# Loading half of the gate's rows early, and moving a quarter of the modal spectrum into the second convolution

## The chip, the cores and the metric

The kernel runs on one core of one Trainium2 chip. The metric is device time in microseconds (us), the median of several executions. The engines are named as the profile names them: PE is TensorE, DVE VectorE, ACT ScalarE, POOL GpSimd and SP SyncE, whose instruction queue issues most of the DMAs.

## The reference

Two layers alternate on x, a sequence of L = 2048 steps with D = 512 channels, twice: A (H3), B (S4D), A, B. Both end in a long causal convolution in each channel, done as a multiplication in the frequency domain with 4096 points.

```python
def _A_ref(q, k, v, shift_k, ssm_k, ssm_D):
    # k_shift: causal convolution of k with 4 taps
    kv = k_shift * v
    y = irfft(rfft(kv, 2*S) * rfft(ssm_k, 2*S))[:S] + kv * ssm_D
    return q * y

def _B_ref(u, log_A_real, A_imag, C_real, C_imag, log_dt, D_skip):
    dt = exp(log_dt); A = -exp(log_A_real) + 1j * A_imag; C = (C_real + 1j * C_imag) * dt
    K = 2.0 * einsum("dn,dnl->dl", C, exp((A * dt) * pos)).real      # the taps, from N = 128 modes
    return irfft(rfft(u, 2*L) * rfft(K, 2*L))[:L] + u * D_skip

x = A_q
x = x + _A_ref(layernorm(x), A_k, A_v, A_shift_k, A_ssm_k, A_ssm_D)
x = x + _B_ref(layernorm(x), B_log_A_real, ..., B_D_skip)
x = x + _A_ref(layernorm(x), A_k, ...)       # the same y as the first time
x = x + _B_ref(layernorm(x), B_log_A_real, ...)
```

Since k and v of layer A are given, its y is the same both times: it is computed once, kept in DRAM (`ya_d`), and each A layer is only an update x = x + layernorm(x) * y.

## The kernel before, in words

Work is cut into 4 quarters of 128 channels (`NQ`) and, in the frequency domain, 8 chunks (`NCH`) per quarter, so that a convolution has 32 steps. A convolution by matmuls goes through these tiles: a first stage of the transform (`fwd_group`: `pf` from `u` or `kk`, L174), a transpose in blocks of 32 on DVE into `zu` or `zk` (L192, L194), a second stage (`f2_chunk`: `pu`, L199), the product with the spectrum `kab` (ACT makes a swapped copy `sw`, L284 and L285; DVE multiplies into `vv`, L286; POOL multiplies `sw`, L288, and adds, L289; every third add is DVE's), a first inverse stage four steps later (`pi`, L298, copied to `ie` by ACT, L299), a transpose into `w` (L313), and a second inverse stage eight steps after that (`po`, L319).

The spectra that these products need are made by the same stages. `spectrum_quarter` makes one quarter of a spectrum: four loads `kk` with a forward group each, then eight chunks that ACT copies from `pu` into `pc` (L250) and SP stores to `spec` in DRAM (L251). It is a generator: each `next` runs one forward group or one chunk. Spectrum 0 belongs to layer A. Spectrum 1, the modal one, belongs to layer B; its taps come from the modes (`taps`: angles, sines `co` on ACT, products `xye`, a contraction on PE, `pk`), which go by way of `kdram` (L549) to `kk`.

The program has three parts that matter here. First, `diagonal()` (spectrum 0 and the convolution of layer A, which stores `ya_d`, L684) runs interleaved with `stream()` (the taps and spectrum 1). Where group 16, 32, 48 or 64 of the taps is contracted, the quarter of spectrum 1 that is then complete is put into the list `todo`, which `stream()` works off. Second, `gated_update` for the first A layer: it loads x (L729) and the rows `yaq` of `ya_d` (L732, in two pieces, groups 0 to 11 and 12 to 15, for the first three of four row blocks), makes `ut` = 1 + y * rs on ACT (L743), updates x on DVE (L754), and takes statistics of the new rows on DVE for the first eight row tiles and as squares on ACT (L760) for the last eight. `normalizer` turns them into `rs` and `nb` with a square root on ACT (L216, behind a load of an activation table) and a short chain on DVE (L217 to L222). Third, the convolution of layer B, `conv_b(0)`: `u` is the normalised x (L817 on ACT, others on DVE), and steps 0 to 31 follow.

Within one engine the instructions run in a fixed order, which the framework's scheduler sets when the program is built; a step of a generator that is written earlier tends to come earlier on every engine. DMAs stand in the queue of the engine that issues them (SP for most, POOL for `kk` of the last quarter and the first two `kab`).

Of the kernel before, what the change touches and what calls it, by code (L numbers as in the profile page):

```python
# [9 lines left out]
F32 = mybir.dt.float32  # L10
# [91 lines left out]
def kernel(ctx: ExitStack, tc: tile.TileContext, out, x_in, kv_in, ssmk_in, ssmd_in,  # L102
# [122 lines left out]

    def spectrum_quarter(which, q, src, pool, zlast, zb, tag):
        z = pool.tile([128, 64, 32, 2], F32, name="zk", tag="z", bufs=zb) if which else z_of_a()
        dr = pool.tile([1, 128], F32, name="dr", tag="dr", bufs=1)
        nc.sync.dma_start(dr, (ssmd_in, dsk_in)[which][:, 128 * q:128 * q + 128])
        for g in range(4):  # L230
            kk = pool.tile([128, 512], F32, name="kk", tag="kk", bufs=3 - which)
            (G if which and q == NQ - 1 else nc.sync).dma_start(kk, src[4 * q + g])
            d = dr[:, 32 * g:32 * g + 32]
            if which == 0:
                kv = kk.rearrange("p (t c) -> p t c", c=32)
                view = lambda ps_, j, n: kv[ps_, :, j:j + n]
            else:
                kv = kk.rearrange("p (i t c) -> p t i c", i=4, c=8)
                view = lambda ps_, j, n: kv[ps_, :, j // 8:(j + n) // 8, :]
                d = d.rearrange("p (i c) -> p i c", c=8)  # L240

            G.tensor_add(kv[0:1, 0], kv[0:1, 0], d)
            fwd_group(view, z, 32 * g, 32, 32 if "f1" in psum else 16, zlast[-zb] if len(zlast) >= zb else None, full="f1" not in psum)
            yield
        for c in range(NCH):
            pu, ins = f2_chunk(z, c, None, tag)
            if c == NCH - 1:
                zlast.append(ins)
            pc = pool.tile([128, CK * 128], F32, name="pc", tag="pc", bufs=2 + 2 * which)
            last_pc[0] = S.copy(pc, pu.rearrange("p k c -> p (k c)"))  # L250
# [215 lines left out]

    NR = 3
    WG = 6
# [91 lines left out]
    def taps():  # L560
# [9 lines left out]
        for n in range(64 + LP + LC):  # L570
# [19 lines left out]
            if 0 <= m < 64:  # L590
                contract(*divmod(m, 4))
                if m % 16 == 15:
                    todo.append(spectrum_quarter(1, m // 16, kdram, kp, zlast_k, 1, "c1"))
# [23 lines left out]
    with ExitStack() as actx:  # L617
# [63 lines left out]
        def finish_a(q, g, po):  # L681
            ya = ap.tile([128, 512], F32, name="ya", tag="pc", bufs=2)
            S.copy(ya, po.rearrange("p t c -> p (t c)"))
            nc.sync.dma_start(ya_d[:, :, 4 * q + g].rearrange("k p x -> p k x"), ya.rearrange("p (k x) -> p k x", k=4))  # L684

        def diagonal():
            kvs = kv_steps()
# [21 lines left out]
            for _ in kvs:  # L709
                yield  # L710
            yield from main

# [12 lines left out]
    def gated_update(buffer, spare, rnd, load_x=False):  # L725
        yas = []
        for k in range(4):
            if load_x:
                nc.sync.dma_start(x[:, 4 * k:4 * k + 4, :], x_in[:, 4 * k:4 * k + 4, :])  # L729
            ya = buffer(k)  # L730
            for lo, hi in ((0, 12), (12, 16)) if rnd == 0 and k < YS else ((0, 16),):
                nc.sync.dma_start(ya[:, lo:hi].rearrange("p g t c -> p (g t c)"), ya_d[k][:, lo:hi].rearrange("p g x -> p (g x)"))  # L732
            yas.append(ya)
# [37 lines left out]
    NKB = 4  # L771
    NSB = 5
    NYA = 3
    YS = 3
# [197 lines left out]
```

## Time and profile before

| | |
|---|---|
| median of 3 executions | 703.12 us (701.06 to 703.45) |
| the profiled execution | 707.13 us |
| its span in the trace | 705.4 us |
| mean granted clock of TensorE | 0.939 |

The span runs from the first to the last instruction of the trace; 1.7 us of the profiled execution lie around it. The profiled execution took 4.0 us more than the median. Times in the rows below are on the clock of that span.

### The profile page before, as it was taken

What the parts mean: (1) busy time and instruction counts of PE and PEld (TensorE: products, weight loads), DVE (VectorE), ACT (ScalarE), POOL (GpSimd) and SP (SyncE); (2) the same over time, 40 slices, a digit from 0 to 9 for tenths busy, and PEclk for the clock granted to TensorE, in tenths of its full rate; (3) what the DMA queues carried; (4) which work ended last, traced back from release to release, by engine and by line L of the source; (5) the groups of instructions that cost most, each with busy time, mean ns of one, the idle gap of its engine ahead of it and who ended that gap; (6) DMA issues with size and microseconds to landing.
All of it is one profiled execution on the core that took longest, in us unless ns stands there. A gap on an engine that the chain in (4) does not pass through costs nothing. (4 is left out here: it accounts for less than half of the span.)

```text
span 705.4 us, 14397 instructions
## 1 busy us (share of the span) xinstructions
PE 574.8 (81%) x5060; PEld 401.1 (57%) x5064; DVE 523.1 (74%) x950; ACT 487.8 (69%) x888; POOL 460.3 (65%) x481
## 2 busy tenths in 40 slices
PE   2297798687889999989887967998998628699995
PEld 0063454445767777757654556767677304476782
DVE  7948979768595875655746785576869897988875
ACT  4346667568779787986979487966665275696572
POOL 4649889679587794984876502187657402787783
PEclk9999999789999999999989989998998959999999
DMA  8678787665756558655581985389676230577682
GB/s 279 206 236 304 235 287 231 219 229 189 238 170 176 143 158 224 185 144 151 156 256 30 300 298 165 120 206 289 162 195 164 75 105 0 151 184 220 188 230 105
DMA packets 83916, 134.10 MB, mean 190 GB/s; under 512 B 16148, under 2 KB 33156, under 8 KB 82692
## 3 DMA queue, kind: packets, MB, share of 16 engines
q1 hardware_dynamic: 82628, 130.75, 62.5%
q0 software_dynamic: 1216, 2.44, 1.3%
q8 instruction: 40, 0.66, 0.4%
q14 instruction: 32, 0.26, 0.1%
HBM read 97.97 MB, written 35.52 MB: 189 GB/s over the span
## 5 line engine op out<-in xcount | busy, mean ns | idle before, releaser
L288 POOL TENSOR_TENSOR sw<-sw,kab 128x512 f32<-128x512 f32 x96 | 124.6, 1303 | 71.7 <-ACT sw L285 68.7
L286 DVE TENSOR_TENSOR vv<-pu,kab 128x512 f32<-128x512 f32 x96 | 65.0, 681 | 66.2 <-ACT sw L285 44.0
L298 PE MATMUL pi<-vv,mm 128*128 128x128 f32 x768 | 106.6, 284 | 3.6 <-DVE vv L286 2.5
L298 PEld LDWEIGHTS pi<-vv,mm 128*128 128x128 f32 x768 | 98.0, 198 | 17.0 <-issue 7.0
L289 POOL TENSOR_TENSOR vv<-vv,sw 128x512 f32<-128x512 f32 x76 | 98.7, 1303 | 9.7 <-DVE vv L286 7.2
L284 ACT ACTIVATE sw<-pu 64x512 f32<-64x512 f32 x96 | 57.0, 594 | 65.0 <-PE pu L199 62.0
L174 PE MATMUL pf<-kk,wz 128*128 128x256 f32 (+1 forms) x176 | 58.9, 580 | 38.8 <-issue 21.2
L523 POOL TENSOR_TENSOR xye<-co,m 128x512 f32<-128x512 f32 x64 | 75.5, 1179 | 22.1 <-ACT co L513 12.8
L635 POOL TENSOR_TENSOR term<-kvt 128x512 f32<-128x512 f32 x64 | 81.5, 1291 | 12.3 <-ACT acc L641 9.8
L199 PEld LDWEIGHTS pu<-zu,w 128*128 128x128 f32 x512 | 66.0, 199 | 40.8 <-DVE vv L286 14.9
L199 PEld LDWEIGHTS pu<-x,w 128*128 128x128 f32 x512 | 70.9, 207 | 28.1 <-ACT pc L250 12.1
L199 PE MATMUL pu<-x,w 128*128 128x128 f32 x512 | 77.1, 296 | 11.5 <-ACT pc L250 8.0
L199 PE MATMUL pu<-zu,w 128*128 128x128 f32 x512 | 76.1, 293 | 9.8 <-DVE vv L286 8.9
L174 PE MATMUL pf<-u,wz 128*128 128x256 f32 (+2 forms) x280 | 76.2, 477 | 4.3 <-DVE zu L192 2.5
L319 PE MATMUL po<-w,w 128*64 128x512 f32 x192 | 53.7, 634 | 9.1 <-DVE w L313 8.1
L511 ACT ACTIVATE co<-pa 128x512 f32<-128x512 f32 x64 | 38.4, 601 | 32.3 <-PE pa L505 22.2
L174 PEld LDWEIGHTS pf<-kk,wz 128*128 128x128 f32 (+1 forms) x176 | 28.0, 211 | 56.9 <-issue 28.1
L494 ACT ACTIVATE m<-pm 128x512 f32<-128x512 f32 x96 | 52.8, 608 | 10.9 <-PE pm L485 7.0
L250 ACT COPY pc<-pu 128x512 f32<-128x512 f32 x64 | 37.0, 585 | 32.3 <-PE pu L199 16.2
L537 PEld LDWEIGHTS pk<-xye 128*32 128x32 f32 x2048 | 36.2, 116 | 36.4 <-issue 18.6
L285 ACT COPY sw<-pu 64x512 f32<-64x512 f32 x96 | 55.5, 578 | 1.1
L524 DVE TENSOR_TENSOR xye<-pa,m 128x512 f32<-128x512 f32 x64 | 43.3, 676 | 16.8 <-ACT pa L512 8.3
(147 smaller groups left out, 1129.9 us busy)
## 6 DMA issues: line engine op xcount, KB each, us to landing
kab<-spec SPq DMA_DIRECT2D x188, 256.0 KB, 4.2
spec<-pc SPq DMA_DIRECT2D x64, 256.0 KB, 3.0
kvt<-kv_in SPq DMA_DIRECT2D x16, 624.0 KB, 4.4
yaq<-ya_d SPq DMA_DIRECT2D x5, 1024.0 KB, 7.0
kk<-ssmk_in SPq DMA_DIRECT2D x16, 256.0 KB, 6.9
kv_d<-un SPq DMA_DIRECT2D x16, 256.0 KB, 2.2
xt<-x_in SPq DMA_DIRECT2D x16, 256.0 KB, 6.3
kdram<-ks SPq DMA_DIRECT2D x64, 64.0 KB, 2.6
```

The source lines that it names most:

```text
L174: yield T.matmul(o, w, rhs, start=True, stop=True)
L199: ins = T.matmul(pu[:, i, :], w2[:, c * CK + i, :], z[:, :, c * CK + i, :], start=True, stop=True)
L284: S.mul(sw[0:64], pu[64:128], -1.0)
L285: swapped[0] = S.copy(sw[64:128], pu[0:64])
L286: multiplied[0] = V.tensor_mul(vv, pu, kabs[s][:, 0])
L288: (V if last else G).tensor_mul(sw, sw, kabs[s][:, 1])
L289: (V if last or s % add_dve == add_dve - 1 else G).tensor_add(vv, vv, sw)
L298: i1s[t] = T.matmul(pi[:, i, :], mm[:, c * CK + i, :], vvs[t][:, i, :], start=True, stop=True)
L319: ins = T.matmul(po[64 * a:64 * a + 64], w4, ws[g][:, :, 16 * a:16 * a + 16, :].rearrange("p x t r -> p t x r"), start=True, stop=True, ti ...
L494: i = S.activation(m, pm.rearrange("p (c i) -> p c i", c=16 if col == 2 else 8), AF.Exp)
L523: G.tensor_mul(xye[:, 0, :, 32:96], co[:, :, 1:65], m[:, :, 32:96])
L635: G.tensor_mul(term, kvt[:, 3 - j:19 - j, :], tap(j))
```

## The change

Two parts of work change their place. Early rows: while the convolution of layer A still runs (at its position `JE` = 38), the pieces of `yaq` that hold groups 0 to 11 are loaded for the first two of the four row blocks, and x for these blocks as well. `gated_update` then loads only groups 12 to 15 of them. Last quarter: the last quarter of spectrum 1 is no longer put into `todo`. It is made once the pools of the second convolution are open: its four forward groups before the convolution's first step, and one of its eight chunks with each step from the second on. Space for it comes from the convolution's own tiles (`ie`, `sw` and `w`), and for the early rows from one row buffer `rw` less (3 to 2), one `pc` less (4 to 3) and one `yaq` less (3 to 2); the buffers of `ut` rise from 7 to 10. As the convolution's own banks are in use by then, the forward groups take the wide form with half the rows to a matmul.

```diff
-    def spectrum_quarter(which, q, src, pool, zlast, zb, tag):
-        z = pool.tile([128, 64, 32, 2], F32, name="zk", tag="z", bufs=zb) if which else z_of_a()
+    def spectrum_quarter(which, q, src, pool, zlast, zb, tag, late=False):
+        zt, pct = (("ie", 2), ("sw", NSB)) if late else (("z", zb), ("pc", PCB if which else 2))
+        z = pool.tile([128, 64, 32, 2], F32, name="zk", tag=zt[0], bufs=zt[1]) if which else z_of_a()
...
-            kk = pool.tile([128, 512], F32, name="kk", tag="kk", bufs=3 - which)
-            (G if which and q == NQ - 1 else nc.sync).dma_start(kk, src[4 * q + g])
+            if not late:
+                kk = pool.tile([128, 512], F32, name="kk", tag="kk", bufs=3 - which)
+            else:
+                if g % 2 == 0:
+                    both = pool.tile([128, 2, 512], F32, name="kk", tag="w", bufs=2)
+                kk = both[:, g % 2]
+            (G if late else nc.sync).dma_start(kk, src[4 * q + g])
...
-            pc = pool.tile([128, CK * 128], F32, name="pc", tag="pc", bufs=2 + 2 * which)
+            pc = pool.tile([128, CK * 128], F32, name="pc", tag=pct[0], bufs=pct[1])
...
-                if m % 16 == 15:
+                if m % 16 == 15 and m < 63:
                     todo.append(spectrum_quarter(1, m // 16, kdram, kp, zlast_k, 1, "c1"))
...
+        def early_rows():
+            for k in range(2):
+                ya = ye.tile([128, 16, 4, 32], F32, name="yaq", tag="yae", bufs=2)
+                nc.sync.dma_start(ya[:, 0:12].rearrange("p g t c -> p (g t c)"), ya_d[k][:, 0:12].rearrange("p g x -> p (g x)"))
+                first_yas.append(ya)
+            if XE:
+                for k in range(2):
+                    nc.sync.dma_start(x[:, 4 * k:4 * k + 4, :], x_in[:, 4 * k:4 * k + 4, :])
...
-            yield from main
+            for j, _ in enumerate(main):
+                if j == JE:
+                    early_rows()
+                yield
...
-            ya = buffer(k)
-            for lo, hi in ((0, 12), (12, 16)) if rnd == 0 and k < YS else ((0, 16),):
+            ya = first_yas[k] if early else buffer(k)
+            for lo, hi in ((12, 16),) if early else ((0, 12), (12, 16)) if rnd == 0 and k < YS else ((0, 16),):
...
-    for _ in first:
-        pass
+    spectrum = spectrum_quarter(1, NQ - 1, kdram, pools["conv"], zlast_k, 1, "c1", True)
+    for _ in range(4):
+        next(spectrum)
+    for j, _ in enumerate(first):
+        if j >= 1:
+            next(spectrum, 0)
```

Of the order in which SP issues its DMAs, this is the stretch at the end of layer A's convolution. Before:

```order
L684 DMA ya_d<-ya 128x4x128
L549 DMA kdram_78<-ks 32x4x128 x4
L684 DMA ya_d<-ya 128x4x128
...
L549 DMA kdram_79<-ks 32x4x128 x2
L732 DMA yaq<-ya_d 128x1536
L732 DMA yaq<-ya_d 128x512
L732 DMA yaq<-ya_d 128x1536
L732 DMA yaq<-ya_d 128x512
L229 DMA dr<-dsk_in 1x128
L732 DMA yaq<-ya_d 128x1536
L732 DMA yaq<-ya_d 128x512
L732 DMA yaq<-ya_d 128x2048
```

And after, where 128x1536 is the piece of 768 KB and 128x512 that of 256 KB:

```order
L696 DMA ya_d<-ya 128x4x128
L701 DMA yaq<-ya_d 128x1536 x2
L558 DMA kdram_78<-ks 32x4x128 x4
L696 DMA ya_d<-ya 128x4x128
...
L558 DMA kdram_79<-ks 32x4x128 x2
L757 DMA yaq<-ya_d 128x512 x2
L757 DMA yaq<-ya_d 128x1536
L757 DMA yaq<-ya_d 128x512
L757 DMA yaq<-ya_d 128x2048
```

The two large pieces of the first two row blocks now stand behind the twelfth store of `ya_d`, and only their small pieces are left behind the last.

On PE, where the second convolution begins (`zk` belongs to spectrum 1, `zu` to the convolution's own data), the order before is this:

```order
L174 MATMUL pf<-kk,wz 128x16x8x2 x16
L199 MATMUL pu<-zk,w_103 128x128 x32
L174 MATMUL pf<-u,wz 128x16x8x2 x16
L199 MATMUL pu<-zu,w_103 128x128 x4
L174 MATMUL pf<-u,wz 128x16x16x2 x2
L199 MATMUL pu<-zu,w_103 128x128 x8
L174 MATMUL pf<-u,wz 128x16x16x2 x2
```

After the change the same place reads:

```order
L176 MATMUL pf<-u,wz 128x16x8x2 x16
L176 MATMUL pf<-kk,wz 128x16x16x2 x4
L201 MATMUL pu<-zu,w_103 128x128 x8
L176 MATMUL pf<-kk,wz 128x16x16x2 x4
L176 MATMUL pf<-u,wz 128x16x16x2 x2
L201 MATMUL pu<-zk,w_103 128x128 x4
L201 MATMUL pu<-zu,w_103 128x128 x4
L176 MATMUL pf<-u,wz 128x16x16x2 x2
L201 MATMUL pu<-zk,w_103 128x128 x4
L201 MATMUL pu<-zu,w_103 128x128 x4
```

The first stage of `u` comes first now; both stages of the last quarter stand behind it, the second one in pieces of four matmuls between the steps.

On ACT, from the first `ut` to the first `sw`, before (squares are L760, copies of the spectrum L250):

```order
L513 ACTIVATE co_246<-co_246,halfpi 128x8x64
L743 ACTIVATE ut<-yaq,rs 128x512 x4
L250 COPY pc<-pu 128x512 x2
L743 ACTIVATE ut<-yaq,rs 128x512 x4
...
L216 ACT_TABLE_LOAD
L216 ACTIVATE rs<-var 128x8 x2
L817 ACTIVATE u<-x,nb,rs 128x128 x8
L250 COPY pc<-pu 128x512 x8
L817 ACTIVATE u<-x,nb,rs 128x128 x32
L284 ACTIVATE sw<-pu 64x512
```

And after:

```order
L768 ACTIVATE ut<-yaq,rs 128x512 x8
L522 ACTIVATE co_249<-co_249,halfpi 128x8x64
L768 ACTIVATE ut<-yaq,rs 128x512 x3
...
L218 ACT_TABLE_LOAD
L218 ACTIVATE rs<-var 128x8 x2
L841 ACTIVATE u<-x,nb,rs 128x128 x40
L292 ACTIVATE sw<-pu 64x512
L293 COPY sw<-pu 64x512
L292 ACTIVATE sw<-pu 64x512
L293 COPY sw<-pu 64x512
L258 COPY pc<-pu 128x512
```

The last sine now follows eight `ut`, and the eight copies of the last quarter come after the second `sw`, one to a step.

## Rows read from the trace of the kernel before

**Rows 1.** The page's first part: busy us of each engine, its share of the span, and its instructions.
```profile
PE 574.8 (81%) x5060; PEld 401.1 (57%) x5064; DVE 523.1 (74%) x950; ACT 487.8 (69%) x888; POOL 460.3 (65%) x481
```

**Rows 2.** Windows around the first gated update: start, end, length, then busy us and number of instructions of PE, PEld, DVE, ACT and POOL, the granted PE clock, the DMA engines' busy share, GB/s.
```profile
370.00:388.00 18.00, 13.93 (x147) 8.29 (x143) 12.23 (x20) 16.28 (x29) 11.69 (x12) 0.91 0.11 30
399.00:407.00 8.00, 6.64 (x111) 5.16 (x111) 4.13 (x8) 3.62 (x7) 5.11 (x7) 1.00 1.01 339
407.00:428.00 21.00, 13.66 (x97) 11.24 (x97) 19.78 (x50) 19.74 (x41) 1.80 (x5) 0.84 0.72 250
450.00:491.00 41.00, 37.49 (x226) 28.32 (x227) 25.80 (x36) 30.57 (x62) 27.29 (x24) 0.92 0.72 197
```

**Rows 3.** ACT's timeline at the turn from the gated update to the second convolution: start, length, and in brackets the idle time ahead of it with what ended it.
```profile
402.51 0.71 ACT L513 ACTIVATE co<-co,halfpi 128x512 f32<-128x512 f32 x1
406.70 2.56 ACT L743 ACTIVATE ut<-yaq,rs 128x512 f32<-128x512 f32 x4 [3.47 <-DMA yaq<-ya_d]
...
427.34 0.20 ACT L760 ACTIVATION_READ_ACCUMULATOR ut<-x,mv 128x1 f32 x1
...
428.86 0.31 ACT L216 ACTIVATE rs<-var 128x8 f32<-128x8 f32 x2
431.13 3.19 ACT L817 ACTIVATE u<-x,nb,rs 128x128 f32<-128x128 f32 x8 [1.97 <-DVE nb L222]
...
442.65 12.41 ACT L817 ACTIVATE u<-x,nb,rs 128x128 f32<-128x128 f32 x32
455.09 0.59 ACT L284 ACTIVATE sw<-pu 64x512 f32<-64x512 f32 x1
```

**Rows 4.** Groups by line from 404 to 435: busy us and mean ns of one, then the idle time ahead of them and what ended most of it.
```profile
L743 ACT ACTIVATE ut<-yaq,rs 128x512 f32<-128x512 f32 x16 | 10.4, 714 | 4.7 <-DMA yaq<-ya_d 4.7
L760 ACT ACTIVATE ut<-x,mv 128x512 f32<-128x512 f32 x8 | 5.7, 724 | 0.0
L250 ACT COPY pc<-pu 128x512 f32<-128x512 f32 x8 | 4.3, 572 | 0.0
```

**Rows 5.** SP's queue at the end of layer A's convolution (start, length of the issuing), and the DMA issues from 395 to 420 (count, KB each, median us from issue to landing).
```profile
364.02 0.37 SPq L684 DMA_DIRECT2D ya_d<-ya  x1
...
395.82 0.39 SPq L684 DMA_DIRECT2D ya_d<-ya  x1
398.73 2.71 SPq L732 DMA_DIRECT2D yaq<-ya_d  x4
...
yaq<-ya_d SPq DMA_DIRECT2D x3, 768.0 KB, 10.4
yaq<-ya_d SPq DMA_DIRECT2D x3, 256.0 KB, 6.5
kk<-kdram SPq DMA_DIRECT2D x1, 256.0 KB, 4.0
```

**Rows 6.** DVE's timeline between the square roots and the first `u`: start and length.
```profile
429.22 0.67 DVE L194 STREAM_TRANSPOSE zk<-pf 128x512 f32<-128x512 f32 x1
...
429.96 0.67 DVE L194 STREAM_TRANSPOSE zk<-pf 128x512 f32<-128x512 f32 x1
430.91 0.19 DVE L222 TENSOR_TENSOR nb<-nm,rs 128x8 f32<-128x8 f32 x1
```

**Rows 7.** PE's timeline from the gated update to the first `po` of the second convolution: start, length, records, idle time ahead.
```profile
419.94 6.37 PE L174 MATMUL pf<-kk,wz 128*128 128x256 f32 x16 [4.38 <-issue]
...
434.67 7.42 PE L199 MATMUL pu<-zk,w 128*128 128x128 f32 x64 [1.55 <-DVE zk L194]
441.92 7.07 PE L174 MATMUL pf<-u,wz 128*128 128x256 f32 x32
449.80 1.16 PE L199 MATMUL pu<-zu,w 128*128 128x128 f32 x8 [0.81 <-DVE zu L194]
450.89 1.13 PE L174 MATMUL pf<-u,wz 64*128 64x512 f32 x4
...
467.36 1.12 PE L174 MATMUL pf<-u,wz 64*128 64x512 f32 x2
...
484.21 2.08 PE L199 MATMUL pu<-zu,w 128*128 128x128 f32 x8 [1.77 <-DVE vv L286]
...
490.83 1.09 PE L319 MATMUL po<-w,w 128*64 128x512 f32 x4
```

**Rows 8.** Windows of half a us, columns as in rows 2; the third number from the end is the granted PE clock.
```profile
424.50:425.00 0.50, 0.50 (x3) 0.41 (x2) 0.50 (x3) 0.50 (x3) 0.30 (x1) 0.50 0.04 16
...
425.50:426.00 0.50, 0.50 (x4) 0.38 (x2) 0.50 (x4) 0.50 (x2) 0.00 (x0) 1.00 1.08 229
...
489.50:490.00 0.50, 0.50 (x4) 0.50 (x4) 0.00 (x0) 0.26 (x1) 0.00 (x0) 0.50 1.02 250
```

**Rows 9.** Timelines of POOL, DVE and PE in the second convolution's first seventeen steps: the waits.
```profile
456.42 2.51 POOL L288 TENSOR_TENSOR sw<-sw,kab 128x512 f32<-128x512 f32 x2 [19.96 <-ACT sw L285]
...
471.56 0.19 POOL L270 MEMSET kab<- 1x128 f32 x1 [2.33 <-DMA kab<-spec]
...
478.81 1.75 DVE L289 TENSOR_TENSOR vv<-vv,sw 128x512 f32<-128x512 f32 x1 [4.67 <-POOL sw L288]
...
532.12 2.07 PE L199 MATMUL pu<-zu,w 128*128 128x128 f32 x8 [3.86 <-DVE vv L286]
```

More of the change, by code (lines that the diff above doesn't have):

```diff
@@ L124 @@
     GL = 2
+    NSB = 5
+    PCB = 3
     LV = 0
@@ L453 @@
     kp = sbuf(gctx, "spec_k")
+    ye = sbuf(gctx, "ye")
     NT = 3
@@ L464 @@
         factors.append(xye)
-    NR = 3
+    NR = 2
     WG = 6
@@ L604, in stream @@
             yield
+    JE = 38
+    XE = 1
+    first_yas = []
     zxp = sbuf(ctx, "zx", "right")
@@ L727, in gated_update @@
         for k in range(4):
-            if load_x:
+            early = load_x and k < 2
+            if load_x and not (early and XE):
                 nc.sync.dma_start(x[:, 4 * k:4 * k + 4, :], x_in[:, 4 * k:4 * k + 4, :])
-            ya = buffer(k)
-            for lo, hi in ((0, 12), (12, 16)) if rnd == 0 and k < YS else ((0, 16),):
+            ya = first_yas[k] if early else buffer(k)
+            for lo, hi in ((12, 16),) if early else ((0, 12), (12, 16)) if rnd == 0 and k < YS else ((0, 16),):
                 nc.sync.dma_start(ya[:, lo:hi].rearrange("p g t c -> p (g t c)"), ya_d[k][:, lo:hi].rearrange("p g x -> p (g x)"))
@@ L771 @@
     NKB = 4
-    NSB = 5
-    NYA = 3
+    NYA = 2
     YS = 3
@@ L788 @@
         normalized(gated_update(lambda k: yp.tile([128, 16, 4, 32], F32, name="yaq", tag="yaq", bufs=NYA),
-                                own + [(yp, "ut", 16 - 4 * NYA)] * (16 - 4 * NYA), 0, True), 0)
+                                own + [(yp, "ut", 7)] * 7, 0, True), 0)
     bq = sbuf(ctx, "conv_q", "right")
```

## The prediction

> **What bounds the kernel now.** The page comes first. TensorE (PE) is busy for 574.8 us, 81% of the span; no other engine is above 74% [rows 1]. That average says where to look, not what an edit is worth, so the windows come next. Around the first gated update three stages have three limits. From 370 to 388 the DMA engines stand almost empty (share 0.11), while ACT is busy 16.28 of 18 us. From 407 to 428 ACT is busy 19.74 of 21 us: that stage goes at ACT's pace. From 450 to 491, the first steps of the second convolution, PE is busy 37.49 of 41 us [rows 2].
>
> ACT's timeline gives the turn from one stage to the next. ACT ends its last sine at 403.2 (402.51 plus 0.71) and then stands 3.47 us for the first rows of `yaq`. The first `ut` starts at 406.70, the two square roots stand at 428.86, and the first `u` at 431.13 [rows 3]. By line, ACT's work between is 10.4 us of `ut`, 4.3 us of `pc` copies and 5.7 us of squares; of the 4.7 us of waiting for `yaq`, 3.47 is that first wait and 1.24 comes later [rows 4]. What PE does behind it is one chain without a gap above 0.9 us: 64 records of `pu` from `zk` (7.42 us), 32 of `pf` from `u` (7.07), then at 449.80 `pu` of step 0, and the first `po` at 490.83 [rows 7]. From there on PE is close to full, so a start that comes earlier by so much should end earlier by so much. I therefore follow this chain alone.
>
> **Term 1, the early rows.** SP issues the twelfth `ya_d` store at 364.02, the last one at 395.82, and the four pieces of `yaq` from 398.73 to 401.4 [rows 5]. In the order after, two pieces of 768 KB and two of x stand far ahead, in the stretch with DMA share 0.11 [rows 2], where they cost nothing that I can see. What the first `ut` still needs is a piece of 256 KB that has no 768 KB piece ahead of it. It is the first of SP's issues there (four in 2.71 us, 0.68 each), out at 399.4. Its flight is not in the trace as such. Bounds: 6.5 us, the median of these pieces behind their large neighbours, and 4.0, that of a 256 KB `kk` load in the same stretch [rows 5]. The new piece has one piece of its own size beside it, so I take 3.8, just under the nearest row: the queue that made 6.5 is what the edit removes. Then `ut` can start at 403.2. ACT in its new order does the last sine (0.71) after the first eight `ut`, and is free at 402.5. (In the rows ACT's stretch ends at 427.54, its last read at 427.34 plus 0.20 [rows 3].) From 406.70 to 427.54 ACT took 20.84 us; without 1.24 us of waits and with the sine that is 20.3. It ends at 403.2 + 20.3 = 423.5 instead of 427.54: **-4.0**. With 6.5 us of flight the start is 405.9 and the end 426.2: -1.3; if the stage is then held by something else, 0. Early x changes nothing, since its loads stood at almost the same place of the queue before.
>
> The Trainium skill, "DMA: Bandwidth & Descriptors", section "Anatomy of one DMA — SWDGE (gpsimd) path", fits a transfer as 2.0 us plus its bytes over 436 KB per us; 256 KB would then be an estimated 2.6 us. By that the piece is there at 402.0, ACT goes on without a wait at 402.5, and the whole is 0.7 us better. The rows speak against it: not one 256 KB transfer of this stretch has so short a median [rows 5].
>
> **Term 2, two transposes.** Between the square roots and `nb` on DVE stand two transposes of `zk`, at 429.22 and 429.96, of 0.67 us each, and `nb` is done only at 431.10 [rows 6]. The change moves all eight of them behind the gated stage. Less what the chain's own small instructions overlapped, that is 1.2 us; the bound below is 0, where another DVE instruction falls into the gap. So the first `u` is at 423.5 + (431.13 - 427.54) - 1.2 = 425.9, the `u` of quarter 0 are done 3.19 us later at 429.1, and `pf` from `u` begins at 429.5.
>
> **Term 3, the work that moves.** Before, 16 `pf` matmuls from `kk` (32 records) and 64 `pu` from `zk` stood ahead of `pf` from `u`; the first lay in ACT's shadow, the second cost its 7.42 us on the chain [rows 7]. After, `pf` from `u` goes first, and the rest is spread over steps 0 to 8. There PE is the bound, so 7.4 us come back. The `pf` from `kk` now comes in the wide form, 16 records: four records of that form took 1.13 us, so 4.4 us in all, all of it new on the chain, half (2.2) ahead of step 0 where it also covers the 0.81 us wait for `zu`. One more pair of `pf` is split; two records alone took 1.12 us, four took 1.13 [rows 7]: +1.1. The eight `pc` copies go from ACT's stretch after `u` into the steps, where ACT has 10 of 41 us free [rows 2]: 0. Moved DMAs: eight spectrum stores of 256 KB go into SP's queue among the `kab` loads, four `kk` loads go ahead of the first `kab` on POOL's queue. In steps of some 3.4 us that is 512 plus 256 KB a step, 226 GB/s; from 450 to 491 the window gives 197 GB/s at share 0.72, so 274 at share 1 [rows 2]. It fits with a fifth to spare: 0, and it is rival R1 if not.
>
> **Term 4, a cold PE.** Here the rows speak against the change. After a gap of 4.38 us PE's `pf` from `kk` at 419.94 took 6.37 us for 16 records, 398 ns each, where the 32 at 441.92 took 221 [rows 7]; the granted clock reads 0.50 at 424.5 (the level of 1.2 GHz) and 1.00 at 425.5 (2.4 GHz) [rows 8]. That dip was hidden behind ACT. After the change PE has next to nothing between some 420 and 429.5, so `pf` from `u` itself meets the low clock. By the rows above the excess is 16 x (398 - 221) = 2.8 us in the one case; I take **+2.6**, bounds 0 (as at 441.92) and 5.7 (all 32 records at 398 ns).
>
> **Term 5, the stall that was there.** Of the 41.03 us from step 0 to the first `po`, 3.5 are PE idle (41 - 37.49), and a second cold stretch lies at the end: 8 records took 2.08 us at 484.21 against 1.16 at 449.80 [rows 7], with the clock still at 0.50 at 489.5 [rows 8]. Six us at that pace hold work of 3.3, an excess of 2.7. So 34.8 us are work and 6.2 are lost. The cause reads back: ACT's 32 `u` (442.65 to 455.06) hold the first `sw` until 455.09 [rows 3], POOL begins only at 456.42 after 19.96 us idle, meets a wait of 2.33 for `kab` of step 8, and DVE's add then waits 4.67 for POOL [rows 9]. After the change the `u` end near 442, when step 0 begins, and each of the first nine steps is longer by the `zk` work, which POOL (1.3 us an instruction) uses to keep up. I expect the 6.2 to go and one small wait to remain, taken as large as the 0.81 for `zu` [rows 7].
>
> **Sum.** 429.5 + 7.07 + 2.6 + 2.2 = 441.4 for step 0 (before 449.80); plus 34.8 + 7.4 + 2.2 + 1.1 + 0.8 = 46.3 gives the first `po` at 487.7 instead of 490.83: -3.1. Behind it the order is the same. The profiled execution took 707.13 us with a span of 705.4; it becomes 704.0. It lies 4.0 above the median of 703.12, of which -3.1 makes **700.0 us**.
>
> **Rivals.** R1, slower: the stores among the `kab` loads, and the shared `sw` buffers (a `pc` must wait for the add two steps back), keep the stall. POOL already waited 2.33 for `kab` at step 8 [rows 9]; if the wait is above 2 us with PE idle, the cold stretch comes as well, and term 5 returns nothing: -3.1 + 6.2 - 0.8 = +2.3, with a longer stall up to +5, so 705 to 708. Against it stands the reserve of a fifth in bandwidth. The Trainium skill, same page, section "Where 436 GB/s comes from", puts the limit between HBM and SBUF at about 358 GB/s for a core; that reserve would then be larger and R1 less likely. The 399 to 407 row (339 GB/s at share 1.01) agrees, the `kab` stage does not get there [rows 2]. R2, no gain: the 256 KB pieces land as late as before (-1.3 in place of -4.0) and the low clock lasts over 20 records (3.5 in place of 2.6); -3.1 + 2.7 + 0.9 = +0.5: 703 to 704. R3, more: the next quarter's stall of 3.86 us at 532.12 with its own 2.07 us cold records [rows 9] vanishes too, since POOL no longer starts late: another 6, so 694. For it speaks that it looks like the first; against it that it is nine steps later, where the old backlog was gone.
>
> **Chances.** Main case 0.58, 697 to 702.5; R1 0.19, R2 0.15, R3 0.08. One can tell 0.5%, 3.5 us, from no change: the main case lies about that line, so 0.33 of it counts as faster and 0.25 as same. R3 makes faster 0.41; R1 gives 0.14 to slower and 0.05 to same, R2 0.13 to same and 0.02 to slower: same 0.43, slower 0.16. The range 694.5 to 706 leaves out part of R3 and of R1.
>
> **What would show it.** ACT's wait before the first `ut` gone or below 1 us (term 1); no transpose between root and `nb` (2); 32 records of `pf` from `u` at above 221 ns with a clock of 0.50 (4); first `po` near 487.7 on that clock, POOL's first product near 443 (pu, then the two halves of `sw`, behind 441.4), no PE gap above 1 us before it (5). Wrong if DVE or POOL waits more than 2 us for `kab`, or the cold stretch outlasts `pf` from `u`.

## The result and the profile after

The changed kernel takes 709.18 us (median of 16 executions) beside 704.88 us for the kernel before, measured together with it; the ratio is 1.0066, with a 95% interval of 1.0039 to 1.0092. The medians are over all executions; this ratio and those below leave out the ones in which a kernel was in its slower state. That is some 4.6 us slower (0.0066 of 704). Forecast were 3.1 us less, and the range ended at 706.

The page's busy line, beside [rows 1], shows PE with 11 us less busy time, and the span 2 us longer all the same:

```profile
PE 563.9 (80%) x5048; PEld 389.0 (55%) x5048; DVE 522.6 (74%) x950; ACT 487.3 (69%) x888; POOL 461.7 (65%) x481
```

ACT's timeline of the changed kernel, and SP's issues of the rows it waits for (start, length, count; in brackets the idle time ahead and what ended it), beside [rows 3, 5]:

```profile
399.20 2.30 SPq L757 DMA_DIRECT2D yaq<-ya_d  x5
...
400.63 0.59 ACT L521 ACTIVATE pa<-pa 128x512 f32<-128x512 f32 x1
403.02 5.01 ACT L768 ACTIVATE ut<-yaq,rs 128x512 f32<-128x512 f32 x8 [1.80 <-DMA yaq<-ya_d]
...
417.47 0.58 ACT L258 COPY pc<-pu 128x512 f32<-128x512 f32 x1 [1.30 <-DMA spec<-pc]
420.10 0.58 ACT L258 COPY pc<-pu 128x512 f32<-128x512 f32 x1 [1.34 <-DMA spec<-pc]
425.90 1.28 ACT L218 ACT_TABLE_LOAD   x1
428.48 15.49 ACT L841 ACTIVATE u<-x,nb,rs 128x128 f32<-128x128 f32 x40 [0.97 <-DVE nb L224]
448.79 0.59 ACT L292 ACTIVATE sw<-pu 64x512 f32<-64x512 f32 x1 [4.83 <-PE pu L201]
```

The first part of a program varies by some us between executions, so kernels are compared from the same event on: the last `pa` sine ahead of the first `ut`, which in the kernel before stands here:

```profile
402.00 0.60 ACT L512 ACTIVATE pa<-pa 128x512 f32<-128x512 f32 x1
```

PE's timeline of the changed kernel, beside [rows 7]:

```profile
435.56 10.19 PE L176 MATMUL pf<-u,wz 128*128 128x256 f32 x32 [18.54 <-ACT u L841]
445.68 1.99 PE L176 MATMUL pf<-kk,wz 64*128 64x512 f32 x8
447.60 2.06 PE L201 MATMUL pu<-zu,w 128*128 128x128 f32 x16
...
453.28 1.13 PE L176 MATMUL pf<-u,wz 64*128 64x512 f32 x4 [1.71 <-DVE zk L194]
...
493.98 1.09 PE L327 MATMUL po<-w,w 128*64 128x512 f32 x4 [0.82 <-ACT ie L307]
...
534.33 2.07 PE L201 MATMUL pu<-zu,w 128*128 128x128 f32 x8 [2.50 <-DVE vv L294]
```

From the last `pa` sine to the first `po` it was 490.83 - 402.00 = 88.8 us before and is 493.98 - 400.63 = 93.4 now: +4.5, the size of the timed difference. These two executions as a whole lie only 2.0 us apart, because the part ahead of the sine came out 1.4 us shorter and the part behind the first `po` 1.2 us shorter. So two single traces put the loss in this stretch, and the experiments have to confirm it; the rows say where to look. `ut` starts early. ACT then waits twice for a buffer of `pc`. The first `u` starts at 428.48, but `pf` from `u` only 7.1 us later, after 18.54 us without work for PE. The windows show what that does to the clock (columns as in [rows 2]): from 426 to 436 PE is busy 0.44 us and the granted clock is 0.50, the level of 1.2 GHz; it is 0.76 on average over the next 12 us and 1.00 (2.4 GHz) from 448 on.

```profile
426.00:436.00 10.00, 0.44 (x1) 0.44 (x2) 3.33 (x19) 9.01 (x23) 4.74 (x12) 0.50 0.89 236
436.00:448.00 12.00, 12.00 (x43) 8.77 (x43) 6.86 (x10) 7.96 (x21) 0.00 (x0) 0.76 0.00 0
448.00:494.00 46.00, 43.47 (x297) 33.10 (x296) 26.60 (x41) 29.08 (x54) 27.19 (x24) 1.00 0.73 210
```

Why is `u` late on PE when ACT has begun it in time? The row "x40" hides an order. With the tiles' numbers, the instruction list of the changed kernel as it was built reads at this place (`u_4792` is quarter 0, `u_4818` quarter 1, `u_4937` quarter 2; neighbours of one tile drawn together):

```
L841 u_4792 x4      quarter 0, the first half of its rows
L841 u_4818 x8      quarter 1
L841 u_4937 x2      quarter 2
L841 u_4792 x4      quarter 0, the second half
L841 u_4818 x8      quarter 1
L841 u_4937 x14     quarter 2
```

`pf` from `u` needs all of quarter 0, so it waits for 18 instructions in place of 8. At 15.49 / 40 = 0.387 us each that is 7.0 us in place of 3.1. The reason stands in `norm` of `steps_b`: `after(i, last_pc[0])` ties the `u` of quarter 1 behind the last `pc` copy that was made when the line runs. In the kernel before that is the last copy of the last quarter, which ACT does after its eight `u` of quarter 0. In the changed kernel that quarter is made later, the last copy known is an early one, and the tie orders nothing. The `u` of quarter 2 have no tie in either kernel; in the kernel before they came last all the same.

### The profile page after: what moved, and what is told of

It reads as the page before. It is cut to its first block, busy times and chain, and to the rows that moved or that the text cites. A ratio compares the mean times of both kernels' runs of the same rounds, so it can differ in the third digit from the quotient of the medians.

```text
span 707.4 us, 14371 instructions
## 1 busy us (share of the span) xinstructions
PE 563.9 (80%) x5048; PEld 389.0 (55%) x5048; DVE 522.6 (74%) x950; ACT 487.3 (69%) x888; POOL 461.7 (65%) x481
## 4 chain that ended last, share of the span: by engine, by line
PE 42%; ACT 17%; DVE 15%; DMA 12%; issue 8%; POOL 4%; SPq 1%; DVEq 0%; ACTq 0%; POOLq 0%
PE pu L201 13%; PE pf L176 12%; PE pi L306 6%; DMA spec<-pc 4%; PE po L327 4%; PE pk L546 3%; ACT co L522 2%; ACT sw L293 2%; ACT sw L292 2%; DMA xt<-x_in 1%; ACT pc L258 1%; PE pm L497 1%; DVE x L779 1%; DMA kab<-spec 1%; ACT co L520 1%
## 5 line engine op out<-in xcount | busy, mean ns | idle before, releaser
L306 PE MATMUL pi<-vv,mm 128*128 128x128 f32 x768 | 103.1, 278 | 2.4 <-DVE vv L294 2.0
L306 PEld LDWEIGHTS pi<-vv,mm 128*128 128x128 f32 x768 | 94.4, 192 | 15.8 <-issue 6.8
L176 PE MATMUL pf<-u,wz 128*128 128x256 f32 (+2 forms) x280 | 80.1, 490 | 24.0 <-ACT u L841 18.5
L201 PEld LDWEIGHTS pu<-zu,w 128*128 128x128 f32 x512 | 62.6, 190 | 36.9 <-DVE vv L294 11.1
L201 PEld LDWEIGHTS pu<-x,w 128*128 128x128 f32 x512 | 68.1, 200 | 26.4 <-ACT pc L258 10.4
L201 PE MATMUL pu<-x,w 128*128 128x128 f32 x512 | 74.5, 290 | 10.0 <-ACT pc L258 6.2
L201 PE MATMUL pu<-zu,w 128*128 128x128 f32 x512 | 72.2, 283 | 8.0 <-DVE vv L294 6.9
L176 PE MATMUL pf<-kk,wz 64*128 64x512 f32 (+1 forms) x160 | 52.8, 605 | 31.9 <-issue 18.2
L176 PEld LDWEIGHTS pf<-u,wz 128*128 128x128 f32 (+1 forms) x280 | 43.3, 196 | 40.7 <-ACT u L841 18.7
L546 PE MATMUL pk<-xye 128*32 128x64 f32 x2048 | 49.9, 234 | 8.3 <-POOL xye L536 6.4
```

The costliest lines, as they stand in the source:

```text
L176: yield T.matmul(o, w, rhs, start=True, stop=True)
L201: ins = T.matmul(pu[:, i, :], w2[:, c * CK + i, :], z[:, :, c * CK + i, :], start=True, stop=True)
L306: i1s[t] = T.matmul(pi[:, i, :], mm[:, c * CK + i, :], vvs[t][:, i, :], start=True, stop=True)
L546: T.matmul(pk[32 * i4:32 * i4 + 32, 2 * k + i, :], xye[:, r, 4 * i + i4, 64:96], xye[:, r, 4 * i + i4, 0:64], start=r == 0, stop=r == 1, t ...
```

## The experiments

The last column is the time as a ratio to the kernel before, measured beside it, with a 95% interval. The others are us of the trace: from the first `ut` to the table load; from the first `u` to `pf` from `u`; length of these 32 records; from `pu` of step 0 to the first `po`; from the first `ut` to the first `po`; and from the last `pa` sine to it, which alone compares kernels with and without early rows. Each is of one execution. In the names, "u_order" stands for the mended order of `u`, "u2" for a tie on the `u` of quarter 2, "yaq" for moved loads, all told below.

| kernel | ut to table | u to pf | pf | step 0 to po | ut to po | pa to po | ratio |
|---|---|---|---|---|---|---|---|
| before | 20.9 | 10.8 | 7.07 | 41.0 | 84.1 | 88.8 | 1 |
| changed | 22.9 | 7.1 | 10.19 | 46.4 | 91.0 | 93.4 | 1.0066 (1.0039 to 1.0092) |
| u_order | 22.7 | 3.2 | 8.85 | 48.3 | 87.6 | 90.1 | 0.9996 (0.9954 to 1.0037) |
| quarter_only | 21.4 | 7.1 | 8.57 | 46.4 | 87.9 | 91.8 | 1.0077 (1.0038 to 1.0115) |
| rows_only | 20.6 | 12.0 | 7.07 | 39.8 | 85.4 | 87.7 | 1.0024 (0.9981 to 1.0066) |
| u_order_kk_sp | 21.9 | 3.2 | 9.58 | 48.0 | 87.2 | 89.0 | 1.0027 (0.9987 to 1.0067) |
| u_order_warm | 23.0 | 10.5 | 7.07 | 46.4 | 91.4 | 93.9 | 1.0275 (1.0220 to 1.0330) |
| u_order_warm9 | 22.8 | 4.1 | 7.07 | 50.7 | 89.1 | 90.5 | 1.0040 (1.0004 to 1.0076) |
| u_order_both | 22.5 | 3.2 | 7.17 | 50.0 | 87.3 | 89.2 | 1.0037 (0.9998 to 1.0075) |
| u_order_one_pc4 | 22.2 | 3.2 | 9.76 | 48.0 | 87.6 | 89.3 | 1.0031 (0.9996 to 1.0067) |
| u2_late | 22.7 | 3.2 | 8.93 | 45.1 | 84.4 | 86.8 | 1.0005 (0.9969 to 1.0040) |
| u2_late_both | 22.7 | 4.1 | 7.07 | 46.3 | 84.7 | 86.2 | 0.9965 (0.9925 to 1.0005) |
| before_u2_late | 21.3 | 10.9 | 7.07 | 37.4 | 81.0 | 85.4 | 0.9977 (0.9943 to 1.0012) |
| rows_u2_late | 20.5 | 10.7 | 7.07 | 36.9 | 81.9 | 84.4 | 0.9974 (0.9933 to 1.0016) |
| before_u2_yaq | 21.8 | 12.5 | 7.07 | 40.1 | 85.9 | 90.7 | 0.9901 (0.9859 to 0.9943) |
| rows_u2_yaq | 20.1 | 12.4 | 7.07 | 36.6 | 81.8 | 83.6 | 0.9922 (0.9880 to 0.9964) |
| u2_both_yaq | 22.5 | 3.2 | 7.17 | 46.4 | 83.7 | 86.3 | 0.9932 (0.9894 to 0.9970) |
| u2_one_kk | 23.2 | 3.2 | 9.55 | 48.3 | 88.7 | 91.1 | 0.9976 (0.9946 to 1.0005) |
| before_yaq | 20.1 | 10.8 | 7.07 | 38.0 | 80.4 | 86.1 | 0.9902 (0.9862 to 0.9941) |
| after_order_yaq | 23.2 | 3.2 | 9.24 | 46.4 | 86.5 | 87.8 | 0.9918 (0.9873 to 0.9963) |

**The order of u.**

```diff
-                    elif rnd == 0 and q == 1:
-                        after(i, last_pc[0])
+                    elif rnd == 0 and q > 0:
+                        after(i, last_root[0])
```

> The changed kernel with one wait of order altered: the u of quarters 1 and 2 stand on ACT behind the last u of quarter 0. Theory 1 (the loss is this order): the eight u of quarter 0 are done 3.2 us after the first one in place of 7.1, pf from u starts near 431.9 in place of 435.56, everything behind comes 3.6 us earlier, the first po near 490.4 in place of 493.98; time some 3.6 us under the changed kernel, so about 1.001 of the kernel before. Theory 2 (the loss is the cold PE and the moved work, the order only sets which engine is waited for): pf from u gives back at its low clock or in later waits what it gains, the first po stays at 493 to 494, time as the changed kernel, 1.006.

ACT and PE in u_order:

```profile
429.65 15.49 ACT L841 ACTIVATE u<-x,nb,rs 128x128 f32<-128x128 f32 x40 [0.97 <-DVE nb L224]
445.15 0.59 ACT L292 ACTIVATE sw<-pu 64x512 f32<-64x512 f32 x1
...
432.88 8.85 PE L176 MATMUL pf<-u,wz 128*128 128x256 f32 x32 [14.47 <-ACT u L841]
443.58 2.05 PE L201 MATMUL pu<-zu,w 128*128 128x128 f32 x16
449.63 1.80 PE L176 MATMUL pf<-u,wz 64*128 64x512 f32 x4 [2.08 <-DVE zk L194]
491.92 1.09 PE L327 MATMUL po<-w,w 128*64 128x512 f32 x4 [0.82 <-ACT ie L307]
```

The same 40 `u`, and `pf` starts 3.2 us behind the first one in place of 7.1. The first `po` stands 3.4 us nearer to the first `ut`; the ratio goes from 1.0066 to 0.9996. Theory 1 holds in the trace, where the one line gives back 3.3 of the 4.5 us counted from the last `pa` sine. In the time it is less sharp: four kernels below that carry the same line and one or two edits more (u_order_kk_sp, u_order_warm9, u_order_both, u_order_one_pc4) stand at 1.0027 to 1.0040. So the line takes back between some 40% and all of the loss in time; how much, these runs don't show. And the 1.3 us that `pf` won beyond that at its clock are gone by the first `po`: step 0 now starts at 443.58, 1.6 us before ACT gets to its first `sw` (1.2 us in the changed kernel, where ACT stands ready), PE then waits 2.08 us for `zk` (1.71), and its clock falls once more, to 0.96 on average from step 0 to the first `po`. In after_order_yaq, of which more below, the same wait is 1.71 us and the clock stays up:

```profile
443.60:491.90 48.30, 45.41 (x298) 34.41 (x296) 26.94 (x41) 30.62 (x58) 27.19 (x24) 0.96 0.70 200
```

```profile
441.60:488.00 46.40, 43.87 (x300) 33.50 (x298) 26.99 (x41) 30.25 (x57) 27.20 (x24) 1.00 0.62 177
```

**Each part alone.** quarter_only puts `yaq`, `ut` and their buffers back; rows_only puts the last quarter back into `todo`, its `kk` loads on POOL's queue as before, and drops the loop's `next(spectrum)`. Both keep the three `pc` and two `rw` buffers.

> Only the late quarter; no early rows, yaq and ut as before. Theory 1: the first ut waits until about 406.7 again, the u stand in the order that splits quarter 0, PE is cold: the first po 2 to 4 us later than in the changed kernel, near 497; ratio 1.009 to 1.012. Theory 2 with the early rows as the cause of the loss: ratio at or below 1.003.

> Only the early rows with their space (one pc and one rw buffer less); the last quarter of the spectrum is made where it was before. The first ut starts at 403.0; the waits of pc for its stores (2.6 us in the changed kernel) stay if they come from the three pc buffers, so ACT's stretch ends 1.5 us earlier than before, some 426. With both transposes in the chain and no cold PE the first po comes at 489.3, 1.5 us earlier than before: ratio 0.998. If ACT waits no more for pc, 487 and 0.995. If the early rows themselves delay something in the first part, 1.000 or more.

quarter_only carries the loss (1.0077, split order, cold PE). But its first `po` was forecast 2 to 4 us later than in the changed kernel and, counted from the last `pa`, comes 1.6 us earlier: its first `ut` starts 1.5 us later behind the sine, but ACT's stretch is 1.5 us shorter, without a wait for `pc`, and `pf` takes 8.57 us. So inside the changed kernel the early rows brought nothing that these traces show. In rows_only the order comes back by itself, since the copies stand between the `u` again. Its first `po` was forecast 1.5 us earlier than before; counted from the last `pa` it comes 1.2 us earlier, and nothing of that is left in the time. ACT waits longer for `nb` there than in the kernel before, 3.51 us in place of 1.97 [rows 3], since the two `zk` transposes between root and `nb` wait for PE themselves:

```profile
426.10 0.72 DVE L196 STREAM_TRANSPOSE zk<-pf 128x512 f32<-128x512 f32 x1 [0.99 <-PE pf L176]
427.63 0.72 DVE L196 STREAM_TRANSPOSE zk<-pf 128x512 f32<-128x512 f32 x1 [0.81 <-PE pf L176]
429.27 3.19 ACT L841 ACTIVATE u<-x,nb,rs 128x128 f32<-128x128 f32 x8 [3.51 <-DVE nb L224]
```

**The cold clock.** Matmuls that nobody reads, behind the last x (`WU1 = 15`, `WX = 18`; then 9, in the first update alone):

> As u_order, with 18 matmuls of 512 columns that nobody reads behind the last x on PE, so that PE doesn't stand idle before pf from u. If the low clock costs what the trace of the changed kernel shows (10.19 us for the 32 records in place of 7.07), pf from u takes 7.1 us again and the first po comes 3 us earlier than in u_order, near 487.4; ratio about 0.997. If the added matmuls still run when u is ready, part of it is lost; if the clock was no cost, the time is that of u_order.

> As u_order, with 9 matmuls nobody reads on PE behind the last x, in the first gated update alone. They run from some 423 to 432 and end about when u is ready. pf from u at the full clock: 7.1 us in place of 8.85; first po 1.8 us earlier counted from the first ut; ratio 0.997 to 0.998. If the clock costs less than its records say, ratio as u_order.

PE in u_order_warm (first two rows of the first update, the third of the second update), then in u_order_warm9:

```profile
425.48 17.36 PE L791 MATMUL idle<-x,wz 128*128 128x512 f32 x36 [4.75 <-ACT ut L785]
442.67 7.07 PE L176 MATMUL pf<-u,wz 128*128 128x256 f32 x32
...
583.43 13.44 PE L791 MATMUL idle<-x,wz 128*128 128x512 f32 x24 [17.23 <-DVE mv L214]
```

```profile
418.57 10.78 PE L791 MATMUL idle<-x,wz 128*128 128x512 f32 x18 [3.47 <-ACT ut L785]
429.19 7.07 PE L176 MATMUL pf<-u,wz 128*128 128x256 f32 x32
488.76 1.09 PE L327 MATMUL po<-w,w 128*64 128x512 f32 x4 [0.82 <-ACT ie L307]
```

The first was mis-sized: 18 matmuls are 36 records of 0.48 us, so they ran 7 us past the last `u` of quarter 0, up to which they should have bridged, and they ran in the second update too, where nothing was to bridge: 1.0275 (1.0220 to 1.0330). Both show `pf` at 7.07 us behind a busy PE, so the 1.8 to 3.1 us are the clock's. But u_order_warm9 is no faster than u_order (1.0040, 0.9996, intervals overlapping): step 0 comes 0.8 us earlier behind the first `ut`, PE then waits 2.98 us for `zk`, the granted clock falls to 0.50 there (446 to 450), and the stretch behind step 0 grows to 50.7 us. The dip was moved, not removed.

**What took it back: ACT, and the clock behind it.** u_order_both, with the clock kept up to `pf` and the `kk` loads moved, shows the chain:

> Both edits together. If the two losses are separate, the first po comes 3.8 to 4 us earlier than in u_order counted from the first ut, 83.6 us in place of 87.6: ratio 0.994 to 0.995. If a freed ACT only waits for another engine, no better than the better of the two.

```profile
445.73 0.59 ACT L292 ACTIVATE sw<-pu 64x512 f32<-64x512 f32 x1
447.00 0.69 DVE L294 TENSOR_TENSOR vv<-pu,kab 128x512 f32<-128x512 f32 x1 [2.73 <-ACT sw L293]
448.75 2.50 DVE L194 STREAM_TRANSPOSE zk<-pf 128x512 f32<-128x512 f32 x4
450.21 1.17 PE L176 MATMUL pf<-u,wz 64*128 64x512 f32 x4 [3.77 <-DVE zk L194]
```

`pu` of step 0 starts at 442.5, yet ACT does `u` without a gap until 445.7. `vv` waits on DVE for `sw`, the last four `zk` transposes stand behind `vv`, PE waits for them 3.77 us, and from 452 to 454 its granted clock is 0.50. ACT is not the whole of it: in u_order_kk_sp and u_order_one_pc4 the first `sw` comes 1.2 us behind `pu`, as in the changed kernel, and the stretch still takes 48.0 us at a mean clock of 0.96. To take ACT out of it, the 16 `u` of quarter 2, which nothing needs yet, were put behind the steps' `sw`, in the changed kernel and in the kernel before:

```diff
-                    if q >= QA:
+                    if q >= (QA if rnd else 2):
```

> As u_order, and the 16 u of quarter 2 are tied on ACT behind sw of the steps, two to a step, instead of standing in one stretch ahead of the first sw. Theory 4 (in u_order PE reaches step 0 before ACT has ended its 40 u, so sw of step 0 waits for ACT, vv and the last four zk transposes wait behind it on DVE, and PE waits for those): the stretch from pu of step 0 to the first po falls from 48.3 us to 45 or 46, first po 84.5 to 85.5 us behind the first ut in place of 87.56; ratio 0.996. Rival (the steps are bound by PE and the DMA of kab anyway): 48 us stay, ratio 1.000.

> As u2_late, with the kk loads on SP's queue and the 9 matmuls that keep PE at the full clock. By theory 4 these two gained nothing before since PE only reached ACT's u earlier; now they should: pf from u 7.1 us, pc waits 2 us or less, first po 82.5 to 83.5 us behind the first ut, ratio 0.993. Rival: as u2_late.

> The kernel before, with only the 16 u of quarter 2 tied behind the steps' sw. The prediction laid the stall between step 0 and the first po (41.0 us, of which 6.2 lost) on ACT's 32 u ahead of the first sw. If that holds, the first sw starts near 450.6 instead of 455.09, the stretch takes 36 to 38 us, the clock does not fall there; ratio 0.994. If the stall is that of kab loads or of POOL's pace, 40 us or more, ratio 0.999 to 1.001.

> As rows_only, with the same tie. If the early rows bring 1.5 us and the tie what it brings in before_u2_late, the first po stands 81 to 82 us behind the first ut in place of 85.4, ratio 0.992. If the tie brings nothing, ratio as rows_only, 1.002.

The first `po` come as theory 4 says: 84.4 in place of 87.6, 81.0 in place of 84.1, 81.9 in place of 85.4 us behind the first `ut`; only u2_late_both, with 84.7, misses its 82.5 to 83.5. In the kernel before the stretch from step 0 falls from 41.0 to 37.4 us. That its stall was ACT's `u`, as the prediction had it, does not follow. Here are the windows from step 0 to the first `po` of before_u2_late, of before_yaq (below), which leaves the `u` where they were, with the first `sw` 5.3 us behind `pu` as in the kernel before, and of before_u2_yaq (below), which has the tie:

```profile
447.50:484.90 37.40, 34.42 (x224) 25.58 (x225) 21.57 (x31) 31.51 (x62) 27.34 (x24) 1.00 0.71 184
```

```profile
447.20:485.20 38.00, 34.76 (x226) 25.52 (x226) 25.02 (x34) 29.60 (x60) 27.23 (x24) 1.00 0.61 153
```

```profile
450.40:490.50 40.10, 37.43 (x224) 26.98 (x224) 24.08 (x34) 31.00 (x62) 27.41 (x24) 0.91 0.61 159
```

With the clock at 1.00 the stretch takes 38.0 us without the tie and 37.4 with it; at 0.91 or 0.92 [rows 2] it takes 40.1 with it and 41.0 without. So of the 3.6 us some 3 are a fall of the clock that one trace has and another has not, whatever ACT does; what decides it is open.

And yet no ratio is below 0.9965, and every interval reaches 1 or past it. In the traces the gain is given back behind the first `po`: from there to the end of the span it is 214.6 us in the kernel before and 219.1 in before_u2_late. POOL's rows there, in before_u2_late:

```profile
481.75 1.27 POOL L288 TENSOR_TENSOR sw<-sw,kab 128x512 f32<-128x512 f32 x1 [2.46 <-DMA kab<-spec]
493.31 0.20 POOL L270 MEMSET kab<- 1x128 f32 x1 [1.42 <-DMA kab<-spec]
522.59 0.19 POOL L270 MEMSET kab<- 1x128 f32 x1 [3.33 <-DMA kab<-spec]
```

**What took that back: loads of 1 MB among those of kab.** Three of the four `yaq` loads for the second gated update stand in SP's queue among the `kab` loads of steps 8 to 24; the fourth comes at 570.91, behind them. In the kernel before (first three rows) and in before_yaq:

```profile
476.09 0.52 SPq L732 DMA_DIRECT2D yaq<-ya_d  x1
...
482.56 0.53 SPq L732 DMA_DIRECT2D yaq<-ya_d  x1
...
511.32 0.37 SPq L732 DMA_DIRECT2D yaq<-ya_d  x1
```

```profile
530.23 1.47 SPq L733 DMA_DIRECT2D yaq<-ya_d  x3
```

They are needed only when this convolution has ended. Tied behind the last `kab` (with `last_kab[0]` set at each `kab` load; "..." stands for the rest of a line):

```diff
-                nc.sync.dma_start(ya[:, lo:hi].rearrange(...
+                ins = nc.sync.dma_start(ya[:, lo:hi].rearrange(...
+                if rnd == 1:
+                    after(ins, last_kab[0])
```

> As before_u2_late, and the four loads of yaq of 1 MB each for the second gated update stand behind the last kab load instead of among the kab loads. Theory 5 (the gain up to the first po is given back because kab loads come late, and these 4 MB are what delays them): the waits for kab between 480 and 535, 9.1 us in before_u2_late, fall to 4 or less, the stretch from the first po to the end of the steps is 3 us shorter; ratio 0.993. Rival (kab loads wait for their own four buffers, so steps and loads pace each other): the waits stay at 7 to 9 us, ratio 0.997 to 0.998.

> As rows_u2_late with the same move of the yaq loads. Theory 5: 3 us less from the first po to the end of the steps; ratio 0.993. Rival: as rows_u2_late, 0.997.

> As u2_late_both with the same move. Theory 5: ratio 0.992. Rival: as u2_late_both, 0.9965.

> The kernel before, with only the yaq loads of the second update behind the last kab. If these loads make the late kab of steps 8 to 24 by themselves, the stall of 3.9 us at step 24 and its cold stretch go: ratio 0.993. If the loads only matter once the steps run faster (tied u), ratio 0.998 to 1.000.

> The changed kernel with the u of quarter 0 first, and the yaq loads moved as in before_yaq. u_order stood equal to the kernel before; if the change has no gain of its own, this one stands equal to before_yaq within 0.3%. If the kab loads were what took back its gain, it is 2 us or more faster than before_yaq.

Waits for `kab` between 480 and 540 (us, times), by tile, in the kernel before, then in before_yaq, then in after_order_yaq:

```profile
  DMA kab<-spec: 7.9, 3
```

```profile
  DMA kab<-spec: 1.2, 2
```

```profile
  DMA kab<-spec: 2.1, 3
```

Theory 5 holds. The move gains 1.0% by itself (before_yaq), with the tied `u` no more than that (before_u2_yaq), and it beats both kernels: some 7 us under the kernel before. From the first `po` to the end of the span it is 207.7 to 210.9 us in the six traces with moved loads and 211.8 to 220.7 in the others of the table (u_order_warm, with matmuls added there too, left out). One of the six gains little in the time: u2_one_kk stands at 0.9976 (0.993 forecast), since its stretch from the last `pa` to the first `po` is 91.1 us. (The trace of before_u2_yaq has its first `po` late, by a stretch of 12.5 us from `u` to `pf` and the low clock behind step 0, and ends early all the same; why the first is so is open.) And the change, with its order mended, stands beside it at 0.9918 against 0.9902, so it has no gain of its own that these runs can tell, with the `kab` loads out of the way.

**The pc waits.** Two attempts to take away ACT's 2.6 us: the `kk` loads of the late quarter on SP's queue (`nc.sync` in place of `G if late else nc.sync`), and one early row block with `PCB = 4`; then both.

> As u_order, but the four kk loads of the late quarter stand on SP's queue behind the spectrum stores instead of on POOL's, where three of them run from 412 on among those stores. Theory 3 (ACT waits for pc because these loads stretch a store to 7.5 us and there are only three pc buffers): the 2.5 us of pc waits fall to 0.5 or less, ACT's stretch from the first ut to the table load takes 20.3 to 20.7 us in place of 22.7, the first po comes 2 us earlier than in u_order; ratio 0.997. Rival (three buffers are too few whatever runs beside the stores): 2 us or more of pc waits stay, ratio as u_order, 1.000.

> As u_order, with one early row block in place of two and four pc buffers again (the kk loads stay on POOL's queue). Theory 3: no pc wait, but the second row block's ut waits for its rows as before, about 1 us: net 1 to 1.5 us earlier than u_order, ratio 0.998. Rival (the pc wait is the kk loads alone, not the buffers): pc waits of 1 us or more remain, ratio 1.001 or more.

> As u2_late with one early row block, four pc buffers, the kk loads on SP's queue and the yaq loads of the second update behind the last kab. If the pc waits had both causes, they are 0.3 us or less here, and the time from the first ut to the table load is 20.3 to 21.5 us with the wait for the second block's rows; ratio 0.993. If a third cause holds them, 0.9 us or more remain.

The waits are 1.76, 0.93 and 2.07 us; the last should have had none, so neither the buffers nor the `kk` loads alone explain them. In the changed kernel three `kk` loads run on POOL's queue from 411 on, and `spec` stores beside them took 7.5 us; in u2_one_kk the next in POOL's queue, four `kab` loads of 256 KB, have taken their place. The first fence is of the changed kernel, issues of 412 to 413, the second of u2_one_kk, 410 to 411:

```profile
kk<-kdram POOLq DMA_DIRECT2D x2, 256.0 KB, 6.2
spec<-pc SPq DMA_DIRECT2D x2, 256.0 KB, 7.5
```

```profile
kab<-spec POOLq DMA_DIRECT2D x2, 256.0 KB, 6.9
```

In rows_only nothing of POOL's queue runs there, the stores land within 4.5 us, and ACT waits 0.48 us. That points at what POOL's queue lets go at this moment, whatever it is. Against it stands quarter_only: three buffers, three `kk` loads on POOL's queue from 407.96 on, and no wait for `pc`; there ACT's own waits for `yaq` (2.71, 0.68 and 1.11 us) space the copies. A run that holds back both loads was not made, nor one that spaces the copies alone, so the cause of these 2.6 us is argued and not shown.

## Why the prediction was wrong

- **Term 1** was right in the number of its row and wrong in the stretch. The first `ut` started at 403.02 (403.2 forecast), 3.8 us after SP began to issue its piece (4.5 forecast). By the Trainium skill, "DMA: Bandwidth & Descriptors", section "Anatomy of one DMA — SWDGE (gpsimd) path", it would have been an estimated 2.6; the row decides. That the start agrees is luck: SP issues the piece only 1.4 us ahead of the last `pa` sine, 3.3 before, so that `ut` starts 2.4 us behind the sine, where the forecast had 1.2 and the kernel before 4.7. And the stretch took 22.9 us, not 20.3: the forecast left out that ACT waits 2.64 us for its spectrum stores.
- **Term 2** was near in size: ACT's wait for `nb` fell from 1.97 to 0.97 us, so 1.0 for the 1.2 forecast.
- **The step that failed** stands at the end of term 2: "the `u` of quarter 0 are done 3.19 us later". I took the length of the eight `u` from the row of before, where they stand alone, and read the row "x40" of the new order as eight and then 32. It hides the tiles. Rows with their numbers would have shown 4, 8, 2, 4, and the code shows why: the copies that were moved away were what the tie hung on. This cost 3.9 us (7.1 from the first `u` to `pf`, 3.2 in u_order), and u_order, with one line altered, has the first `po` 3.3 us earlier, counted from the last `pa`.
- **Term 4** was right in kind and near in size: 10.19 - 7.07 = 3.1 us (2.6 forecast). In the six kernels with the order mended and no added matmuls it is 1.8 to 2.7.
- **Term 3** and **term 5** came out together at 46.4 us from step 0 to the first `po` (46.3 forecast), by luck as to their parts. "The `u` end near 442, when step 0 begins" held only because step 0 came 6 us late, and the granted clock stayed at 1.00 behind it. Where step 0 came in time, it was 48.0 to 50.7 us with a clock of 0.93 to 0.97 (u_order and the four kernels like it), and 46.4 with 1.00 (after_order_yaq). Of the 6.2 us that term 5 laid on ACT's `u`, some 3 are absent from before_yaq, where the `u` stand as before and the clock does not fall; so the cause that it read back is not shown.
- **The end.** That an earlier first `po` is carried to the end was wrong in the traces that had one: before_u2_late gained 3.4 us there and lost 4.5 behind it; its time is 0.2% less, with 1 inside the interval. The late `kab` loads of R1 were the right mechanism for this, but at steps 8 to 24, in both kernels alike (7.9 and 8.0 us of waits between 480 and 540), so they are not what made the change slower; and their cause was not the spectrum stores but three loads for a later stage. R3 did not come either: the stall of the next quarter still stands at 534.33, 2.50 us and then 8 records in 2.07. The limit of about 358 GB/s, with which the prediction took chance from R1, stood in no term; in quarter_only the window from 408 to 416 has 412 GB/s, so the row of 339 did not mark a limit.

Against the forecast of -3.1 the stretch from the last `pa` sine came out at +4.5: a miss of 7.6. Of it 3.5 lie between the first `u` and `pf` (7.1 us, 3.6 forecast), 2.6 in ACT's stretch (the `pc` waits), and 1.2 in the start of `ut`; the rest is small terms.

## What to carry to other kernels

When work is moved away, look for the waits and ties that were hung on it: an order that was kept by the moved instruction is lost without any line of the diff saying so, and a grouped row of equal instructions can hide it. A gain counts only if the next engine in line is free at the new time, so after each step of the sum ask which engine ends last there now. And a load for a later stage that sits in the queue among those of the present one is worth moving first: here an edit of a few lines gave 1.0%, some 7 us, where the whole change was meant to give 3.1. And before a stall is laid on an engine, compare a trace in which the clock did not fall: here two traces of nearly the same stretch differed by 3 us, almost all of it the clock.

## What the runs showed of the hardware

In the changed kernel, a 256 KB store that lands in 2.0 us in a quiet moment (420 to 422) took 7.5 us with three 256 KB loads beside it (412 to 413). After 10.78 us of matmuls that nobody reads, 32 `pf` records took 7.07 us; after 18.54 us without work they took 10.19, with the granted clock at 0.50 ahead of them. Removing that one low stretch gained nothing that could be measured (u_order_warm9 1.0040, u_order 0.9996): behind it PE waited 2.98 us in place of 2.08, and the clock was at 0.50 again from 446 to 450. From step 0 to the first `po` of the kernel before and its kin, the stretch took 38.0 us or less where the granted clock was 1.00, and 39.8 to 41.0 where it was 0.91 to 0.96.
